# Order of the output and of the opening terms in the first MoE of a fused attention and MoE kernel

## Chip, cores and metric

The kernel runs on one core of one Trainium2 chip. The metric is the device time of one execution in microseconds (us); lower is better.

## What is computed

```python
def reference(q, k, v, f, ...):
    # attention: B=4, H=8, S=576, D=64
    s = q @ k^T / sqrt(D) + decay(f)           # decay: differences of cumsum(log f); causal
    x = softmax(s) @ v                         # then rows (B*S, H*D) = (2304, 512)
    # first MoE, d_ff 768
    h = maximum(maximum(x @ w1, x @ w2), x @ w3)
    x = h @ w_out                              # (2304, 512)
    # second MoE, d_ff 2048
    h = x @ w_in
    P = a[0] + a[1]*h + a[2]*h*h + a[3]*h*h*h
    Q = 1 + |b[0]|*|h| + |b[1]|*h*h
    return (P / (Q + 1e-6)) @ moe2_w_out
```

## The kernel before

Every product of two fp32 matrices is made of a high and a low part of each operand: three matmuls (high with low, high with high, low with high) are summed in PSUM, the accumulator of TensorE, which has eight banks. The x, hh and xo below therefore are pairs: ACT copies the sum to the high part, and VectorE (or GpSimd) subtracts that from the sum, which gives the low part.

**Attention.** Heads go in pairs, four to a batch (hp 0 to 3). The 576 queries of a batch fall in two groups g, of 320 and 256 columns (GQ). A unit is one head of a pair in one group. One step of the main loop works on three units: scores of the newest (L388, L389, two banks of ps_s; VectorE L390 adds the mask and frees the bank, ACT L396 takes the exponential), transposes of the one before (L428, three banks of ps_t), product with v of the one before that (L444, one bank of ps_o). After a pair's second head, ACT L451 and VectorE L452 make x, one tile for each head pair dc, batch and group. tk and tq (L335) are transposes of keys and queries of a later pair.

**First MoE.** For each batch and group there are 22 units of work (moe1_units): 18 of moe1_h, for six chunks fc of d_ff and three weights j, and four of moe1_o, one for each part dc of the 512 output rows. A unit of moe1_h has 12 matmuls (four head pairs, three terms: L476, L477, L478) on a bank of ps_h, which has two. ACT L482 copies the first weight's result to m, VectorE L484 takes the maximum with the second and third; then ACT L488 and GpSimd (VectorE in the tail, L490) make the chunk's hh. A unit of moe1_o has 18 matmuls on x2p (six chunks, three terms: L502, L503, L504), an eviction to xo (ACT L507, VectorE L508; xo has two buffers), and a store to x2d in DRAM (L57). The function fill hands these units out between the steps of the attention of the next batch. The order that each engine then runs is set by a scheduler, which works on the written order; so a written change moves instructions on all engines.

**Tail.** The last batch's two groups (b = 3) have no attention beside them. tail["n"] is set at L649: hbank then takes banks of four kinds in turn. Beside these units w_in is converted to a high and a low part, in 32 pieces, two for each of 16 column blocks: SP loads a piece (L167, a ring of six buffers), ACT L181 takes the magnitude, VectorE does four steps (L186, L187, L188, L191), ACT L197 copies the high part, GpSimd L200 makes the low one. **Second MoE.** It follows (hq, L732 to L734; oo, L781 to L783), with x2h and x2l and x loaded from x2d.

The two places that the change touches, as they were:

```python
for dc in reversed(range(NDC)):        # moe1_h: newest head pair first
...
for fc in range(NF1):                  # moe1_o: one part dc, all six chunks
```

Of the kernel before, what the change touches and what calls it, by code (L numbers as in the profile page):

```python
# [9 lines left out]
F32R = mybir.dt.float32r  # L10
# [14 lines left out]
GQ = [(0, 320), (320, 576)]  # L25
# [12 lines left out]
def kernel(  # L38
    ctx: ExitStack, tc: tile.TileContext, q, k, v, f, w1, w2, w3, w_out, m2_in, m2_out, m2_a, m2_b, out
):  # L40
    nc = tc.nc
# [4 lines left out]
    P = 128  # L46
    NDC = DM // P
    NF1 = FF1 // P
# [4 lines left out]
    def r32(ap):  # L53
        return ap.bitcast(F32)

    def move(dst, src):
        return nc.sync.dma_start(r32(dst), r32(src))  # L57
# [4 lines left out]
    mpool = ctx.enter_context(tc.tile_pool(name="mpool", bufs=1, side="left"))  # L62
# [47 lines left out]
    for a, z in GQ:  # L110
        part = slice(a, z)
# [350 lines left out]
    def hbank(name):  # L462
        pool, tag = ps_h, "h"
        if tail["n"] is not None:
            pool, tag = TAILP[tail["n"] % len(TAILP)]
            tail["n"] += 1
        return pool.tile([P, 512], F32, name=name, tag=tag)

    def moe1_h(b, g, fc, j):
        w = GQ[g][1] - GQ[g][0]  # L470
        nm_ = f"{b}_{g}_{fc}"
        xs = [xt[b, dc, g] for dc in range(NDC)]
        wh, wl = w1t[fc]
        hp_ = hbank(f"h{j}_{nm_}")
        for dc in reversed(range(NDC)):
            nc.tensor.matmul(hp_[:, :w], wh[:, j, dc], xs[dc][:, 1], start=(dc == NDC - 1), stop=False)  # L476
            nc.tensor.matmul(hp_[:, :w], wh[:, j, dc], xs[dc][:, 0], start=False, stop=False)  # L477
            nc.tensor.matmul(hp_[:, :w], wl[:, j, dc], xs[dc][:, 0], start=False, stop=(dc == 0))  # L478
        with tc.high_priority():
            nxt = mpool.tile([P, 320], F32, name=f"m{j}_{nm_}", tag="mx", bufs=3)  # L480
            if j == 0:
                nc.scalar.activation(nxt[:, :w], hp_[:, :w], AF.Copy)  # L482
            else:
                nc.vector.tensor_tensor(nxt[:, :w], cur[0][:, :w], hp_[:, :w], op=ALU.max)  # L484
            cur[0] = nxt
            if j == 2:
                hh = mpool.tile([P, 2, 320], F32R, name=f"hh_{nm_}", tag="hh", bufs=6)
                nc.scalar.activation(hh[:, 0, :w], nxt[:, :w], AF.Copy)  # L488
                eng = nc.gpsimd if tail["n"] is None else nc.vector
                eng.tensor_tensor(hh[:, 1, :w], nxt[:, :w], r32(hh[:, 0, :w]), op=ALU.subtract)  # L490
                hs[b, g, fc] = hh

    def moe1_o(b, g, dc):
        lo, hi = GQ[g]
        w = hi - lo
        nm_ = f"{b}_{g}_{dc}"
        xp = hbank(f"x2p_{nm_}")
        ds_ = slice(dc * P, (dc + 1) * P)
        for fc in range(NF1):
            hh = hs[b, g, fc]  # L500
            woh, wol = wot[fc][:, 0, ds_], wot[fc][:, 1, ds_]
            nc.tensor.matmul(xp[:, :w], woh, hh[:, 0, :w], start=(fc == 0), stop=False)  # L502
            nc.tensor.matmul(xp[:, :w], wol, hh[:, 0, :w], start=False, stop=False)  # L503
            nc.tensor.matmul(xp[:, :w], woh, hh[:, 1, :w], start=False, stop=(fc == NF1 - 1))  # L504
        with tc.high_priority():
            xo = mpool.tile([P, 2, 320], F32R, name=f"xo_{nm_}", tag="xo", bufs=2)
            nc.scalar.activation(xo[:, 0, :w], xp[:, :w], AF.Copy)  # L507
            nc.vector.tensor_tensor(xo[:, 1, :w], xp[:, :w], r32(xo[:, 0, :w]), op=ALU.subtract)  # L508
            move(x2d[:, dc, :, b * S + lo : b * S + hi], xo[:, :, :w])

    def moe1_units(b, g):
        return [lambda fc=fc, j=j: moe1_h(b, g, fc, j) for fc in range(NF1) for j in range(3)] + [
            lambda dc=dc: moe1_o(b, g, dc) for dc in range(NDC)
        ]


# [83 lines left out]
    for step in range(len(slots) + 2):  # L600
# [4 lines left out]
        if u is not None and u.pair.n + 1 < len(pairs):  # L605
            n = u.pair.n + 1
# [4 lines left out]
        if o:  # L611
            o.attend()
            if step in ready:
                queue.append((step, [x for bg in ready[step] for x in moe1_units(*bg)]))
# [82 lines left out]
    a0, a1, a2, a3, b0, _, b1, one = (ab[:, i : i + 1] for i in range(8))  # L697
# [161 lines left out]
```

## Time and profile before

| what | us |
|---|---|
| median of 3 runs | 954.58 |
| lowest, highest | 954.29, 955.71 |
| profiled execution | 954.83 |
| its span | 953.0 |
| TensorE busy | 932.1 |
| VectorE busy | 723.2 |
| ACT busy | 649.0 |
| GpSimd busy | 239.7 |

The span runs from the first instruction to the last; the 1.8 us between it and the time of the execution lie around it. A busy time is the time in which an engine worked at anything. PE is TensorE, DVE is VectorE, POOL is GpSimd, SPq is the queue in which SP issues transfers. The mean granted clock of TensorE is 0.995. The first MoE of batch 3 runs from about 475 to 554 us, the second MoE from there to the end.

### The profile page before, as it was taken

Reading aid. Unit: us, or ns where it says so; the run is one execution under the profiler, and the core shown is the slowest. Engines: PE = TensorE matmul, PEld = TensorE weight load, DVE = VectorE, ACT = ScalarE, POOL = GpSimd, SP = SyncE. Lnnn points to the kernel's source line nnn. Section 1 sums busy time; section 2 is a strip of 40 time slices with the busy share of each in tenths; the row PEclk is TensorE's granted clock in tenths of the full one; section 3 lists DMA queues with packets and bytes.
Section 4 is the critical chain, followed back from the end, with each engine's and each line's share of the span. In section 5 each row is a group of like instructions: output and inputs, shape, how many; then the busy total and the mean of one; then the engine's idle time right before and its main releaser. Section 6 shows DMA issues by size and latency. Waiting matters only on the chain.

```text
span 953.0 us, 16820 instructions
## 1 busy us (share of the span) xinstructions
PE 932.1 (98%) x5780; PEld 825.9 (87%) x5780; DVE 723.2 (76%) x1692; ACT 649.0 (68%) x1542; POOL 239.7 (25%) x392
## 2 busy tenths in 40 slices
PE   6999999999999999999999999999999999999998
PEld 4768899988999999999999988888888888899997
DVE  8578865556777776524397969888988988899996
ACT  6798777777777677546354567667666666777765
POOL 4344444444555455414132400000000000000000
PEclk9988999999999999999999999999999999999999
DMA  7864332123555564220245386011002102100000
GB/s 192 218 191 119 98 84 58 44 77 107 154 148 167 153 174 140 75 78 2 72 140 188 122 300 231 1 45 45 0 1 67 45 1 67 44 1 1 34 1 34
DMA packets 125743, 88.53 MB, mean 93 GB/s; under 512 B 74573, under 2 KB 110425, under 8 KB 125657
## 3 DMA queue, kind: packets, MB, share of 16 engines
q1 hardware_dynamic: 125656, 87.45, 30.6%
q8 instruction: 46, 0.75, 0.3%
q14 instruction: 41, 0.33, 0.1%
HBM read 64.73 MB, written 22.69 MB: 92 GB/s over the span
## 4 chain that ended last, share of the span: by engine, by line
PE 79%; DVE 12%; ACT 5%; issue 2%; DMA 2%; SPq 0%; ACTq 0%; DVEq 0%
PE hq L734 7%; PE oo L782 7%; PE oo L783 7%; PE hq L732 7%; PE hq L733 7%; PE oo L781 7%; PE h L476 5%; PE h L477 5%; PE h L478 5%; PE tp L428 5%; PE o L444 5%; PE s L388 2%; PE s L389 2%; PE x2p L502 2%; PE x2p L504 2%
## 5 line engine op out<-in xcount | busy, mean ns | idle before, releaser
L476 PE MATMUL h<-x,w1h 128*128 128x320 f32 (+1 forms) x576 | 175.4, 305 | 2.1 <-DVE x L452 1.3
L477 PE MATMUL h<-x,w1h 128*128 128x320 f32 (+1 forms) x576 | 171.8, 298 | 0.0
L478 PE MATMUL h<-x,w1l 128*128 128x320 f32 (+1 forms) x576 | 171.3, 298 | 0.0
L476 PEld LDWEIGHTS h<-x,w1h 128*128 128x128 f32 x576 | 109.3, 190 | 4.0 <-DVE m L484 1.9
L782 PE MATMUL oo<-wp,gh 128*128 128x512 f32 x288 | 112.6, 391 | 0.0
L781 PE MATMUL oo<-wp,gh 128*128 128x512 f32 x288 | 112.0, 389 | 0.0
L741 ACT ACTIVATE s<-hq 128x512 f32<-128x512 f32 (+1 forms) x80 | 44.3, 554 | 97.3 <-PE hq L734 97.2
L477 PEld LDWEIGHTS h<-x,w1h 128*128 128x128 f32 x576 | 109.3, 190 | 0.7 <-issue 0.5
L478 PEld LDWEIGHTS h<-x,w1l 128*128 128x128 f32 x576 | 109.1, 190 | 0.2 <-issue 0.2
L783 PE MATMUL oo<-wp,gl 128*128 128x512 f32 x288 | 109.1, 391 | 0.0
L396 ACT ACTIVATE e<-e,st 128x64 f32<-128x64 f32 (+4 forms) x160 | 88.9, 557 | 28.9 <-DVE st L390 26.5
L408 POOL TENSOR_SCALAR e<-e,rs 128x64 f32<-128x64 f32 (+4 forms) x144 | 76.2, 545 | 80.7 <-DVE rs L402 71.0
L390 DVE CUSTOM_DVE_ANT_0 e<-s,mask 128x320 f32<-128x320 f32 (+3 forms) x160 | 67.2, 432 | 32.4 <-PE s L389 21.2
L430 ACT ACTIVATE pt<-tp 128x384 f32<-128x384 f32 (+3 forms) x160 | 70.3, 469 | 15.3 <-PE tp L428 14.2
L744 DVE SCALAR_TENSOR_TENSOR s<-s,ab,u 128x512 f32<-128x512 f32 (+1 forms) x80 | 55.7, 697 | 32.2 <-ACT u L742 32.0
L428 PE MATMUL tp<-ident,e 128*128 128x128 f32 (+1 forms) x480 | 77.0, 279 | 0.0
L734 PE MATMUL hq<-x,wil 128*128 128x512 f32 (+1 forms) x192 | 69.8, 364 | 0.0
L732 PE MATMUL hq<-x,wih 128*128 128x512 f32 (+1 forms) x192 | 69.8, 363 | 0.0
L733 PE MATMUL hq<-x,wih 128*128 128x512 f32 (+1 forms) x192 | 69.6, 363 | 0.0
L783 PEld LDWEIGHTS oo<-wp,gl 128*128 128x128 f32 x288 | 54.1, 188 | 11.3
L782 PEld LDWEIGHTS oo<-wp,gh 128*128 128x128 f32 x288 | 54.0, 188 | 10.6
L781 PEld LDWEIGHTS oo<-wp,gh 128*128 128x128 f32 x288 | 54.1, 188 | 10.4
(133 smaller groups left out, 2433.7 us busy)
## 6 DMA issues: line engine op xcount, KB each, us to landing
raw_w<-in_moe_w_dram SPq DMA_DIRECT2D x18, 512.0 KB
raw_wp<-in_moe_w_out_dram SPq DMA_DIRECT2D x32, 256.0 KB
wpd<-wp SPq DMA_DIRECT2D x32, 256.0 KB
raw_wi<-in_moe_w_in_dram SPq DMA_DIRECT2D x32, 256.0 KB
wp<-wpd SPq DMA_DIRECT2D x10, 768.0 KB
x2d<-xo SPq DMA_DIRECT2D x16, 320.0 KB
out_dram<-ob SPq DMA_DIRECT2D x18, 256.0 KB
kn<-in_k_dram SPq DMA_DIRECT2D x32, 128.0 KB
```

Of the source, the lines that this page charges most:

```text
L396: nc.scalar.activation(e[:nr], e[:nr], AF.Exp, bias=m, scale=-1.0, accum_out=l)
L408: nc.gpsimd.tensor_scalar(e, e, self.rs[:, 1, j : j + 1], 0.0, op0=ALU.mult, op1=ALU.add)
L428: nc.tensor.transpose(tp[:kr, dst : dst + P], self.e[i][:, Q0[c] : Q1[c]], ident)
L476: nc.tensor.matmul(hp_[:, :w], wh[:, j, dc], xs[dc][:, 1], start=(dc == NDC - 1), stop=False)
L477: nc.tensor.matmul(hp_[:, :w], wh[:, j, dc], xs[dc][:, 0], start=False, stop=False)
L478: nc.tensor.matmul(hp_[:, :w], wl[:, j, dc], xs[dc][:, 0], start=False, stop=(dc == 0))
L732: nc.tensor.matmul(hp_[:, :w], wih[:, dc, fs], xh, start=(dc == 0), stop=False)
L733: nc.tensor.matmul(hp_[:, :w], wih[:, dc, fs], xl, start=False, stop=False)
L734: nc.tensor.matmul(hp_[:, :w], wil[:, dc, fs], xh, start=False, stop=(dc == NDC - 1))
L781: nc.tensor.matmul(o, g[0][:, ts_], wh_, start=(fc == 0), stop=False)
L782: nc.tensor.matmul(o, g[0][:, ts_], wl_, start=False, stop=False)
L783: nc.tensor.matmul(o, g[1][:, ts_], wh_, start=False, stop=(fc == NF2 - 1))
```

## The change

It has two parts. In moe1_h, the unit that opens a batch from the second on (first group, first chunk, first weight) takes its 12 terms in the opposite order: oldest head pair first, and of the newest one the term with x's low part last. Units of the output work differently: moe1_out(b, g, 0) makes chunks 0 to 4 of parts 0 and 1, moe1_out(b, g, 1) makes chunk 5 of both and evicts them, and the third and fourth make parts 2 and 3 as before. Lines behind the change are four higher in moe1_h, and L502 to L504, L507 and L508 become L506 to L508, L516 and L517.

```diff
--- before.py
+++ after.py
@@ -472,10 +472,12 @@
         xs = [xt[b, dc, g] for dc in range(NDC)]
         wh, wl = w1t[fc]
         hp_ = hbank(f"h{j}_{nm_}")
-        for dc in reversed(range(NDC)):
-            nc.tensor.matmul(hp_[:, :w], wh[:, j, dc], xs[dc][:, 1], start=(dc == NDC - 1), stop=False)
-            nc.tensor.matmul(hp_[:, :w], wh[:, j, dc], xs[dc][:, 0], start=False, stop=False)
-            nc.tensor.matmul(hp_[:, :w], wl[:, j, dc], xs[dc][:, 0], start=False, stop=(dc == 0))
+        opens = b > 0 and (g, fc, j) == (0, 0, 0)
+        terms = [t_ for dc in reversed(range(NDC)) for t_ in ((wh, dc, 1), (wh, dc, 0), (wl, dc, 0))]
+        if opens:
+            terms.reverse()
+        for n, (w_, dc, part) in enumerate(terms):
+            nc.tensor.matmul(hp_[:, :w], w_[:, j, dc], xs[dc][:, part], start=(n == 0), stop=(n == len(terms) - 1))
         with tc.high_priority():
             nxt = mpool.tile([P, 320], F32, name=f"m{j}_{nm_}", tag="mx", bufs=3)
             if j == 0:
@@ -490,27 +492,47 @@
                 eng.tensor_tensor(hh[:, 1, :w], nxt[:, :w], r32(hh[:, 0, :w]), op=ALU.subtract)
                 hs[b, g, fc] = hh
 
-    def moe1_o(b, g, dc):
-        lo, hi = GQ[g]
-        w = hi - lo
-        nm_ = f"{b}_{g}_{dc}"
-        xp = hbank(f"x2p_{nm_}")
+    xps = {}
+
+    def moe1_o(b, g, dc, fcs):
+        w = GQ[g][1] - GQ[g][0]
+        if fcs[0] == 0:
+            xps[dc] = hbank(f"x2p_{b}_{g}_{dc}")
+        xp = xps[dc]
         ds_ = slice(dc * P, (dc + 1) * P)
-        for fc in range(NF1):
+        for fc in fcs:
             hh = hs[b, g, fc]
             woh, wol = wot[fc][:, 0, ds_], wot[fc][:, 1, ds_]
             nc.tensor.matmul(xp[:, :w], woh, hh[:, 0, :w], start=(fc == 0), stop=False)
             nc.tensor.matmul(xp[:, :w], wol, hh[:, 0, :w], start=False, stop=False)
             nc.tensor.matmul(xp[:, :w], woh, hh[:, 1, :w], start=False, stop=(fc == NF1 - 1))
+
+    def moe1_x(b, g, dc):
+        lo, hi = GQ[g]
+        w = hi - lo
+        xp = xps[dc]
         with tc.high_priority():
-            xo = mpool.tile([P, 2, 320], F32R, name=f"xo_{nm_}", tag="xo", bufs=2)
+            xo = mpool.tile([P, 2, 320], F32R, name=f"xo_{b}_{g}_{dc}", tag="xo", bufs=2)
             nc.scalar.activation(xo[:, 0, :w], xp[:, :w], AF.Copy)
             nc.vector.tensor_tensor(xo[:, 1, :w], xp[:, :w], r32(xo[:, 0, :w]), op=ALU.subtract)
             move(x2d[:, dc, :, b * S + lo : b * S + hi], xo[:, :, :w])
 
+    def moe1_out(b, g, n):
+        every = range(NF1)
+        if n == 0:
+            for dc in range(2):
+                moe1_o(b, g, dc, every[:-1])
+        elif n == 1:
+            for dc in range(2):
+                moe1_o(b, g, dc, every[-1:])
+                moe1_x(b, g, dc)
+        else:
+            moe1_o(b, g, n, every)
+            moe1_x(b, g, n)
+
     def moe1_units(b, g):
         return [lambda fc=fc, j=j: moe1_h(b, g, fc, j) for fc in range(NF1) for j in range(3)] + [
-            lambda dc=dc: moe1_o(b, g, dc) for dc in range(NDC)
+            lambda n=n: moe1_out(b, g, n) for n in range(NDC)
         ]
```

In the lists of the order that follow, a row is an instruction, or some alike, as its engine meets them: line, operation, output, inputs, shape. A name's last number counts the tiles; those ahead of it are group and chunk (hh), group and part (x2p, xo), batch, group and chunk (h, m), head and group (o, x), or the column block of w_in (cv_wi, raw_wi).

TensorE at the opening of batch 1, before, from o of the last head pair on:

```order
L444 MATMUL o_1_0_3016<-pt_128,v_2724 64x320 x2
L444 MATMUL o_1_0_3016<-pt_128,v_2724 64x256 x2
L444 MATMUL o_1_0_3016<-pt_128,v_2724 64x128 x2
L335 MATMUL tq_0_2962<-ident,qn_2621 128x128 x3
L476 MATMUL h_1_0_0_3223<-x_1_0_3023,w1h_173 128x320
L477 MATMUL h_1_0_0_3223<-x_1_0_3023,w1h_173 128x320
L478 MATMUL h_1_0_0_3223<-x_1_0_3023,w1l_174 128x320
L476 MATMUL h_1_0_0_3223<-x_1_0_2636,w1h_173 128x320
```

and with the change, first behind the last output matmuls of batch 0, then from the same o on:

```order
L508 MATMUL x2p_1_3_3131<-hh_1_5_2949,wo_1441 128x256
L480 MATMUL h_1_0_0_3223<-x_1_0_1912,w1l_174 128x320
L480 MATMUL h_1_0_0_3223<-x_1_0_1912,w1h_173 128x320 x2
L480 MATMUL h_1_0_0_3223<-x_1_0_2249,w1l_174 128x320
L480 MATMUL h_1_0_0_3223<-x_1_0_2249,w1h_173 128x320 x2
L480 MATMUL h_1_0_0_3223<-x_1_0_2636,w1l_174 128x320
L480 MATMUL h_1_0_0_3223<-x_1_0_2636,w1h_173 128x320 x2
L444 MATMUL o_1_1_2798<-pt_130,v_2342 64x256 x8
```

```order
L444 MATMUL o_1_0_3025<-pt_128,v_2724 64x320 x2
L444 MATMUL o_1_0_3025<-pt_128,v_2724 64x256 x2
L444 MATMUL o_1_0_3025<-pt_128,v_2724 64x128 x2
L335 MATMUL tq_0_2962<-ident,qn_2621 128x128 x3
L388 MATMUL s_1_11_1_1_3077<-k1s_1370,q1s_1432 128x256
L389 MATMUL s_1_11_1_1_3077<-k2s_1371,q2s_1433 128x256
L480 MATMUL h_1_0_0_3223<-x_1_0_3032,w1l_174 128x320
L480 MATMUL h_1_0_0_3223<-x_1_0_3032,w1h_173 128x320
L335 MATMUL tq_1_2972<-ident,qn_2621 128x128 x2
L480 MATMUL h_1_0_0_3223<-x_1_0_3032,w1h_173 128x320
L480 MATMUL h_1_0_0_3265<-x_1_0_3032,w1h_173 128x320 x2
```

Nine of the opening unit's terms moved ahead of o_1_1; behind o_1_0 and tq_0 now stand two scores, two terms with x's high part, two transposes, and the term with the low part.

VectorE in the tail, first group of batch 3, from the second maximum of the last chunk on, before:

```order
L484 TENSOR_TENSOR m_3_0_5_7141<-m_3_0_5_7106,h_3_0_5_7128 128x320
L191 SCALAR_TENSOR_TENSOR cv_wi_8_7279<-raw_wi_8_7191,cv_wi_8_7279 128x256
L484 TENSOR_TENSOR m_3_0_5_7176<-m_3_0_5_7141,h_3_0_5_7163 128x320
L490 TENSOR_TENSOR hh_0_5_7178<-m_3_0_5_7176,hh_0_5_7178 128x320
L508 TENSOR_TENSOR xo_0_0_7220<-x2p_0_0_7201,xo_0_0_7220 128x320
L508 TENSOR_TENSOR xo_0_1_7263<-x2p_0_1_7244,xo_0_1_7263 128x320
L508 TENSOR_TENSOR xo_0_2_7306<-x2p_0_2_7287,xo_0_2_7306 128x320
```

and with the change:

```order
L486 TENSOR_TENSOR m_3_0_5_7141<-m_3_0_5_7106,h_3_0_5_7128 128x320
L191 SCALAR_TENSOR_TENSOR cv_wi_8_7279<-raw_wi_8_7191,cv_wi_8_7279 128x256
L186 TENSOR_SCALAR cv_wi_8_7312<-cv_wi_8_7312 128x256
L187 TENSOR_SCALAR cv_wi_8_7312<-cv_wi_8_7312 128x256
L186 TENSOR_SCALAR cv_wi_9_7322<-cv_wi_9_7322 128x256
L188 SCALAR_TENSOR_TENSOR cv_wi_8_7312<-raw_wi_8_7233,cv_wi_8_7312 128x256
L486 TENSOR_TENSOR m_3_0_5_7176<-m_3_0_5_7141,h_3_0_5_7163 128x320
L187 TENSOR_SCALAR cv_wi_9_7322<-cv_wi_9_7322 128x256
L191 SCALAR_TENSOR_TENSOR cv_wi_8_7312<-raw_wi_8_7233,cv_wi_8_7312 128x256
L188 SCALAR_TENSOR_TENSOR cv_wi_9_7322<-raw_wi_9_7243,cv_wi_9_7322 128x256
L492 TENSOR_TENSOR hh_0_5_7178<-m_3_0_5_7176,hh_0_5_7178 128x320
L191 SCALAR_TENSOR_TENSOR cv_wi_9_7322<-raw_wi_9_7243,cv_wi_9_7322 128x256
```

Eight conversion steps of blocks 8 and 9 moved ahead of xo_0_0, four of them between the two m, three between the last m and hh_0_5.

SP's queue in the tail, where those blocks are loaded, before:

```order
L167 DMA raw_wi_8_7191<-in_moe_w_in_dram 128x2x256
L57 DMA x2h_1_7872<-x2d 128x512
L57 DMA x2l_1_7873<-x2d 128x512
L57 DMA x2h_2_7876<-x2d 128x512
L57 DMA x2l_2_7877<-x2d 128x512
L57 DMA x2d<-xo_0_0_7220 128x2x320
L57 DMA x2d<-xo_0_1_7263 128x2x320
L167 DMA raw_wi_8_7224<-in_moe_w_in_dram 128x2x256
L167 DMA raw_wi_9_7234<-in_moe_w_in_dram 128x2x256
L167 DMA raw_wi_9_7267<-in_moe_w_in_dram 128x2x256
```

and with the change:

```order
L167 DMA raw_wi_8_7191<-in_moe_w_in_dram 128x2x256
L167 DMA raw_wi_8_7233<-in_moe_w_in_dram 128x2x256
L167 DMA raw_wi_9_7243<-in_moe_w_in_dram 128x2x256
L57 DMA x2h_1_7872<-x2d 128x512
L57 DMA x2l_1_7873<-x2d 128x512
L57 DMA x2h_2_7876<-x2d 128x512
L57 DMA x2l_2_7877<-x2d 128x512
L57 DMA x2d<-xo_0_0_7256 128x2x320
L57 DMA x2d<-xo_0_1_7263 128x2x320
L167 DMA raw_wi_9_7267<-in_moe_w_in_dram 128x2x256
L167 DMA raw_wi_10_7277<-in_moe_w_in_dram 128x2x256
```

The second load of block 8 and the first of block 9 moved ahead of the loads of x2h and x2l and of the stores of xo_0_0 and xo_0_1.

## Rows read from the trace of the kernel before

**Rows 1.** The page: span, and each engine's busy time and instructions.
```profile
span 953.0 us, 16820 instructions
...
PE 932.1 (98%) x5780; PEld 825.9 (87%) x5780; DVE 723.2 (76%) x1692; ACT 649.0 (68%) x1542; POOL 239.7 (25%) x392
```

**Rows 2.** By stretches: us, busy PE, PEld, DVE, ACT, POOL, PEclk, DMA, GB/s.
```profile
500.00:525.00 25.00, 23.45 (x172) 23.07 (x170) 17.89 (x47) 11.16 (x29) 6.94 (x9) 1.00 0.59 188
525.00:550.00 25.00, 23.52 (x190) 22.70 (x189) 23.52 (x63) 12.20 (x34) 9.69 (x13) 1.00 0.35 108
575.00:600.00 25.00, 25.00 (x112) 20.70 (x111) 23.94 (x38) 18.65 (x31) 0.00 (x0) 1.00 0.46 171
```

**Rows 3.** TensorE's waits, 127 to 954 us: sum, times, longest.
```profile
PE x2p L502 <- ACT hh L488: 2.3, 3, 1.5
PE h L476 <- DVE x L452: 1.3, 1, 1.3
PE x2p L502 <- DVE xo L508: 0.9, 2, 0.6
PE x2p L504 <- DVE hh L490: 0.7, 1, 0.7
PE s L388 <- DVE st L390: 0.4, 2, 0.2
```

**Rows 4.** Timeline, opening of batch 1: start, us, engine, instruction, [idle before <- releaser].
```profile
211.99 0.49 DVE L390 CUSTOM_DVE_ANT_0 e<-s,mask 128x320 f32<-128x320 f32 x1
...
220.22 0.77 ACT L396 ACTIVATE e<-e,st 128x576 f32<-128x576 f32 x1
...
220.98 0.43 ACT L451 ACTIVATE x<-o 128x320 fp32r<-128x320 f32 x1
...
221.44 0.49 DVE L452 TENSOR_TENSOR x<-o,x 128x320 fp32r<-128x320 f32 x1 [0.65 <-ACT x L451]
...
221.99 0.42 PE L476 MATMUL h<-x,w1h 128*128 128x320 f32 x1 [1.31 <-DVE x L452]
```

**Rows 5.** Timeline of PE, batch 1, first group, output part 2.
```profile
285.21 0.41 PE L502 MATMUL x2p<-hh,wo 128*128 128x320 f32 x1 [0.63 <-DVE xo L508]
```

**Rows 6.** Timeline, tail, batch 3, first group: output and last hh.
```profile
504.35 0.31 PE L502 MATMUL x2p<-hh,wo 128*128 128x320 f32 x1
...
504.50 0.31 PE L503 MATMUL x2p<-hh,wo 128*128 128x320 f32 x1
...
509.14 0.47 DVE L484 TENSOR_TENSOR m<-m,h 128x320 f32<-128x320 f32 x1
...
509.65 0.47 ACT L488 ACTIVATE hh<-m 128x320 fp32r<-128x320 f32 x1
...
510.15 0.67 DVE L490 TENSOR_TENSOR hh<-m,hh 128x320 fp32r<-128x320 f32 x1 [0.54 <-ACT hh L488]
...
510.17 0.42 PE L502 MATMUL x2p<-hh,wo 128*128 128x320 f32 x1 [1.54 <-ACT hh L488]
```

**Rows 7.** Timelines of SP's queue, ACT and DVE: loads of w_in, conversion behind them.
```profile
478.41 23.36 SPq L167 DMA_DIRECT2D raw_wi<-in_moe_w_in_dram  x12
...
513.25 2.43 SPq L167 DMA_DIRECT2D raw_wi<-in_moe_w_in_dram  x4
...
516.84 0.44 ACT L181 ACTIVATE cv_wi<-raw_wi 128x256 f32<-128x256 f32 x1 [1.66 <-DMA raw_wi<-in_moe_w_in_dram]
...
517.32 0.29 DVE L186 TENSOR_SCALAR cv_wi<-cv_wi 128x256 f32<-128x256 f32 x1 [1.60 <-ACT cv_wi L181]
```

**Rows 8.** Two conversion steps, 475 to 550 us: ns min/median/max, starts, form.
```profile
L186 DVE TENSOR_SCALAR cv_wi<-cv_wi x31: 278/284/870, 475.3 to 544.2; 128x256 f32<-128x256 f32 x31
...
L188 DVE SCALAR_TENSOR_TENSOR cv_wi<-raw_wi,cv_wi x32: 409/425/970, 475.5 to 545.9; 128x256 int32<-128x256 int32 x32
```

**Rows 9.** Timeline of PE, tail, batch 3, second group: first and last output matmul.
```profile
542.76 0.28 PE L502 MATMUL x2p<-hh,wo 128*128 128x256 f32 x1
...
553.78 0.28 PE L504 MATMUL x2p<-hh,wo 128*128 128x256 f32 x1
553.90 0.40 PE L732 MATMUL hq<-x2h,wih 128*128 128x512 f32 x1
```

## Prediction

> **What bounds the kernel now.** I read the page's totals first: TensorE is busy for 932.1 of 953.0 us [rows 1], so no order of the same matmuls can take more than its idle time, and all the matmuls stay. Then the table by stretches: in the second MoE TensorE has no gap at all (25.00 of 25.00), in the tail of the first MoE it has 1.55 and 1.48 us of them in two stretches of 25 us, at the full granted clock of 1.00, 2.4 GHz [rows 2]. The time there is lost to waits, not to the clock. Third, the list of TensorE's waits from 127 us on, which is the part of the program that is reordered: 2.3 + 1.3 + 0.9 + 0.7 + 0.4 = 5.6 us in nine waits [rows 3]. The list counts the idle time ahead of an instruction; the start of a matmul behind a wait is late by some 0.16 us more than that (1.54 listed, 1.70 late, worked out below), so nine waits cost about 7 us. That is the whole stake, 0.7% of the kernel. Last the timelines around those waits. The smallest difference that a measurement here can tell from none is about 0.2%, 1.9 us.
>
> **What the change leaves alone.** TensorE runs the same 5780 matmuls, and the copies, subtractions and transfers are the same in number; only the order differs. TensorE's pitch from one 320-column matmul to the next is 504.50 − 504.35 = 0.15 us whatever bank it writes [rows 6]; changing banks every 15 matmuls I cost at nothing. The second MoE keeps its order and has no gap to fill, so what the first MoE gives or takes comes through to the end in full.
>
> **The opening of a batch.** Before, batch 1's first unit starts with the newest head pair's low part. The chain is: ACT ends an exponential of 0.77 us, copies o to x (220.98, 0.43), VectorE subtracts (221.44, 0.49), and the matmul starts at 221.99 after 1.31 us of idling, late by about 1.5 [rows 4]. In the change nine of the unit's twelve terms (1.3 us of matmuls) stand some 8 us earlier, and behind o of the last head pair come three transposes, two score matmuls (0.12 each, the pitch for 256 columns [rows 9]) and two terms that need only ACT's copy, then two transposes, and the low part last. ACT's copy now precedes the last exponential of 0.77, so x's two parts come that much sooner, while TensorE, having done its nine terms already, also arrives 1.3 sooner, with 0.3 of scores to cover. My hand count of the new wait is 0.3 to 1.1; a **gain of 0.9** (0.4 to 1.4). Batches 2 and 3 open in the same new order, but no wait of L476 other than batch 1's is in the list [rows 3], so they are worth nothing.
>
> **Side by side, outside the tail.** What the pair wants to hide is the last chunk's hh. But none of the L502 waits on hh before the tail: the three add up to 2.3, of which the tail has 1.54 at 510.17 and two smaller ones near the end [rows 3, 6]. The cover from the last h matmul to the first use of hh's last chunk (matmuls between them in the two orders, times the pitch) grows there from 3.5–5.4 us to 4.7–7.0, which buys nothing. What can go wrong is at the bank: parts 0 and 1 now end together, so part 2 waits for an eviction that started later. In batch 0 the stretch between the end of part 0 and the start of part 2 shrinks from 2.2 to 1.3 us for the first group of queries; it was idle for 0.3 there (0.9 less the 0.63 of batch 1 [rows 3, 5]), and ACT and VectorE keep the order of that eviction, so I leave it unchanged. In batch 1's first group, where part 2 was idle for 0.63 us behind VectorE's xo [rows 5], the list now puts a slot's scores and transposes ahead of it (7.2 us instead of 2.0). That wait goes, but nine score groups now stand close together on two banks, each freed by a VectorE step such as the 0.49 us one of [rows 4], where TensorE writes a pair of scores in some 0.3 (two pitches). Nine steps of 0.49 against nine of 0.3 is 1.7 late, less what stands between: I take 2.0 for the new stalls of the whole group against 1.3 now, a **loss of 0.7** (0 to 1.6). In batch 1's second group the scores spread out and the two waits on VectorE's st, 0.4 [rows 3], go: a **gain of 0.4** (0 to 0.5).
>
> **Tail, batch 3, first group.** Before, the output starts at 504.35 and 28 matmuls of 0.147 last until 508.47; the first use of hh's last chunk starts at 510.17, 1.70 late. It waits for VectorE's m (509.14, 0.47) and ACT's hh (509.65, 0.47); hh's low part follows at 510.15 [rows 6]. The change adds two matmuls of cover (0.29). But it pulls eight conversion steps of w_in ahead on VectorE, four between the last two m (behind an L191 that stood there already), three before hh's low part and one right behind it. L186, L187, L186 and L188 thus precede the last m, and the L186 on piece 9 needs that piece's load. SP now issues two of these loads before the x2h and x2l loads, where before they stood behind the stores of xo. SP's earlier loads went out every 23.36 / 12 = 2.0 us and the last ended at 478.41 + 23.36 = 501.8; so by the ring's pace I put the two at 503.7 and 505.7. From issue to ACT's first step took 516.84 − 513.25 = 3.6, and that step 0.44 [rows 7]: piece 9 is ready near 509.8. Then L186 and L188 (medians 0.284 and 0.425 [rows 8]) and m: 510.5 to 511.1 for its start plus copying, against 509.14, hence hh 1.1 to 1.5 later. TensorE has used 0.29 of that; hh's low part stands behind three more steps (some 1.1 us) and costs another 0.3. A **loss of 1.4** (0.7 to 2.4).
>
> **Tail, second group.** From 542.76 to 553.90 pass 11.14 us for 72 matmuls at the pitch 553.90 − 553.78 = 0.12, 8.64 [rows 9]: 2.5 us are waits on hh. VectorE is the late one: it is busy for 23.52 of 25 us [rows 2]. It lost its time earlier: in the stretch before, it worked 17.89 of 25 us, with 1.66 us on ACT and then 1.60 on VectorE spent waiting for the load issued at 513.25 [rows 7]. With the loads out 8 us earlier, VectorE has eight steps of 0.28 to 0.43 (2.9 us) behind it by 520. That lead is more than the 2.5 us, so hh is ready in time: a **gain of 2.4** (1.0 to 2.5). For small shifts elsewhere between 127 and 545 us, where every engine's order differs, I add **0.3** (−0.3 to +1.1), two waits of the size of the smaller ones in [rows 3].
>
> **The sum:** −0.9 + 0.7 − 0.4 + 1.4 − 2.4 + 0.3 = −1.3 us. The profiled execution took 954.83 us, 1.8 outside the span of 953.0; the median of the runs is 954.58, so the sum gives 953.5 on the first and **953.3** on the second.
>
> **The rivals.** (1) *The targets all hit.* The score cluster of batch 1 is spread by what stands between, the loads for piece 9 land in time, and TensorE is served at once: −1.4 − 0.6 − 0.5 − 0.2 − 2.5 + 0.5 = −4.7, that is 949.9. For it: rows show that both tail waits hang on VectorE's backlog, and the change works it off. Against: VectorE's list puts more ahead of the first group's hh, not less. It decides from piece 9 ready by 508.5. Chance 0.22. (2) *Waits only change place.* VectorE's lead is used up by ACT's and GpSimd's part of the conversion, so that the second group gains 1.0 rather than 2.4: +0.1, 954.7. For it: ACT and GpSimd do steps of every piece too, and VectorE's stand behind ACT's. Against: VectorE's 7 idle us of 500 to 525 are largely one late load [rows 2, 7]. Chance 0.15. (3) *The load becomes the bound, and it is slower.* In VectorE's queue a step on piece 9 now precedes the last m. If its buffer comes free, or the transfer lands, 2.4 us later than I put it (512.2 rather than 509.8), VectorE stands still with m behind it, hh and TensorE with it: the first group loses 3.8 instead of 1.4, and of VectorE's lead 0.5 are left, so the second gains 0.5: −0.9 + 0.7 − 0.4 + 3.8 − 0.5 + 0.3 = +3.0, 957.6. It is slower by what can be told from about 511.5 on. For it: DMA is at its densest in the tail right here, 0.59 [rows 2], and the wait for a load of the same kind was 1.66; against: the pace and landing of the earlier loads. Chance 0.14. (4) *VectorE's steps stretch.* L186 takes 0.284 in the median but up to 0.870, L188 up to 0.970 [rows 8]; GpSimd is busy for 6.94 of 25 us there [rows 2], so about two of eight steps would meet it and lose 0.6 each: −1.3 + 1.2 = −0.1, 954.5. It decides by how many of the eight are long. Chance 0.08. The Trainium skill, page "SBUF — State Buffer", section "Who interferes with whom", has VectorE and GpSimd share a pair of ports as an exclusive lock, the second of two such instructions blocked until the first ends; the long L186 and L188 agree with it. By that rule, were all eight blocked, the first group would lose some 4.7 more; the medians at the minimum say that most are not.
>
> **How the numbers follow.** My forecast has the chance 0.41; its own range, from the bounds of its terms taken half way, is 951.6 to 955.0. Of it a third lies below 952.7, two thirds within 0.2%. With rival 1 wholly faster, rivals 2 and 4 mostly the same, and most of rival 3 slower: faster 0.14 + 0.22 = 0.36; same 0.27 + 0.14 + 0.08 + 0.01 = 0.50; slower the remaining 0.14. The range reaches from rival 1 to short of rival 3's full price: 950.0 to 956.6.
>
> **What would show it.** Right: the wait of L476 (now L480) on VectorE's x below 1 us; L502 (now L506) on hh near 547 gone and the last x2p within 8.8 us of the first; at 510, a longer wait than 1.54; VectorE well above 17.89 of 25 us in 500 to 525; a load of piece 9 before 507. Wrong: the second group's waits still there with VectorE earlier; new waits of several us on st in batch 1; any wait inside the second MoE.

## The result and the profile after

| | median us | lowest, highest | runs |
|---|---|---|---|
| before | 955.47 | 954.29, 957.81 | 6 |
| changed | 960.29 | 959.60, 961.30 | 6 |

The change makes the kernel slower: ratio 1.0052, 95% interval 1.0041 to 1.0064, some 4.9 us. Forecast were 953.3 us and a range up to 956.6. The profiled execution of the changed kernel took 960.78 us. Its page:

```profile
span 959.0 us, 16819 instructions
...
PE 935.4 (98%) x5780; PEld 826.6 (86%) x5780; DVE 721.7 (75%) x1692; ACT 647.2 (67%) x1542; POOL 238.2 (25%) x392
```

Against [rows 1], TensorE is *busier* by 3.3 us with the same 5780 matmuls, and the span is longer by 6.0. The first is a sign of the clock: a matmul at the lower clock counts as busy for longer. TensorE's waits from 127 us on (sum, times, longest), to be held against [rows 3]:

```profile
PE s L388 <- DVE st L390: 2.8, 6, 0.7
PE x2p L506 <- ACT hh L490: 2.5, 2, 1.7
PE h L480 <- ACT x L451: 0.7, 1, 0.7
PE tp L428 <- POOL e L408: 0.7, 2, 0.4
PE h L480 <- DVE m L486: 0.5, 1, 0.5
```

The wait of the scores for VectorE's st grew from 0.4 to 2.8 us. Where, the table by stretches says (busy PE, PEld, DVE, ACT, POOL, then PEclk), 275 to 310 us, the outputs of batch 1's first group, of the kernel before:

```profile
275.00:310.00 35.00, 34.33 (x267) 31.93 (x264) 26.73 (x85) 26.26 (x77) 18.12 (x33) 1.00 0.54 160
```

and of the changed one:

```profile
275.00:310.00 35.00, 32.29 (x225) 28.18 (x225) 26.23 (x87) 25.09 (x76) 18.78 (x34) 0.95 0.52 153
```

Idle time of 0.67 us became 2.71, and the clock's mean fell to 0.95. The timeline of PE there, changed kernel:

```profile
284.98 0.36 PE L388 MATMUL s<-k1s,q1s 128*128 128x192 f32 x1 [0.65 <-DVE st L390]
...
287.00 0.36 PE L388 MATMUL s<-k1s,q1s 128*128 128x192 f32 x1 [0.68 <-DVE st L390]
...
290.70 0.47 PE L388 MATMUL s<-k1s,q1s 128*128 128x448 f32 x1 [0.44 <-DVE st L390]
...
291.98 0.49 PE L388 MATMUL s<-k1s,q1s 128*128 128x320 f32 x1 [0.61 <-DVE st L390]
...
292.66 3.59 PE L444 MATMUL o<-pt,v 128*64 128x256 f32 x20
```

The first four rows are of the ten score groups that stand closely together, from 284.98 to 292.26 us (the prediction counted nine). VectorE, ahead of the first of them, was at this:

```profile
279.21 1.12 DVE L191 SCALAR_TENSOR_TENSOR cv_wp<-raw_wp,cv_wp 128x256 int32<-128x256 int32 x1
...
282.47 0.68 DVE L186 TENSOR_SCALAR cv_wp<-cv_wp 128x256 f32<-128x256 f32 x1
283.19 0.29 DVE L187 TENSOR_SCALAR cv_wp<-cv_wp 128x256 int32<-128x256 int32 x1
283.51 0.43 DVE L188 SCALAR_TENSOR_TENSOR cv_wp<-raw_wp,cv_wp 128x256 int32<-128x256 int32 x1
283.98 0.42 DVE L191 SCALAR_TENSOR_TENSOR cv_wp<-raw_wp,cv_wp 128x256 int32<-128x256 int32 x1
284.43 0.48 DVE L390 CUSTOM_DVE_ANT_0 e<-s,mask,st 128x256 f32<-128x256 f32 x1
```

The step that frees a bank of scores, 0.48 long, stands behind a whole piece of the conversion of the second MoE's output weights (wp, by the same lines as that of w_in). The second wait (287.00) comes a step later: the score step that frees its bank stands on VectorE behind L402, which waited for ACT, and ACT had stood for 3.71 us at its own part of the conversion:

```profile
284.48 0.42 ACT L197 ACTIVATE wp<-cv_wp 128x256 fp32r<-128x256 f32 x1 [3.71 <-DVE cv_wp L191]
...
286.38 0.17 DVE L402 RECIPROCAL rs<-rs 128x2 f32<-128x2 f32 x1 [0.53 <-ACT rs L401]
286.46 0.47 DVE L390 CUSTOM_DVE_ANT_0 e<-s,mask 128x320 f32<-128x320 f32 x1
```

And then, by stretches of 2 us, the clock:

```profile
290.00:292.00 2.00, 0.95 (x5) 0.37 (x4) 2.00 (x10) 2.00 (x8) 0.00 (x0) 1.00 0.00 0
292.00:294.00 2.00, 2.00 (x9) 1.10 (x10) 2.00 (x10) 2.00 (x7) 1.90 (x4) 0.54 0.39 139
294.00:296.00 2.00, 2.00 (x16) 1.22 (x12) 0.86 (x3) 1.25 (x5) 2.00 (x5) 0.60 0.35 115
296.00:298.00 2.00, 2.00 (x20) 1.83 (x17) 0.49 (x2) 0.77 (x3) 1.12 (x2) 1.00 0.71 221
```

From 284 to 292 TensorE was busy for 5.28 of 8 us (1.21, 1.32, 1.80 and this 0.95); behind that the granted clock went to its lower level, 1.2 GHz, and the 20 matmuls of o took 3.59 us. In the kernel before the same 20 took 2.17:

```profile
293.72 2.17 PE L444 MATMUL o<-pt,v 128*64 128x256 f32 x20
```

So 1.4 us of the loss is the clock's on this group alone.

**Lost time.** To compare kernels whose order differs, I add up, over all matmuls, the distance from its start to the next start less the median distance behind a matmul of the same kind in the kernel before. That counts waits and the lower clock alike, in us:

| kernel | 218–275 | 275–310 | 310–475 | 475–572 | ratio (95%) |
|---|---|---|---|---|---|
| before | 2.8 | 2.2 | 3.9 | 4.3 | |
| changed | 3.7 | 6.3 | 5.4 | 3.6 | 1.0052 (1.0041–1.0064) |
| e1 opening alone | 3.6 | 4.8 | 5.1 | 4.6 | 1.0051 (1.0033–1.0069) |
| e2 side by side alone | 3.1 | 3.6 | 4.6 | 7.0 | 1.0029 (1.0015–1.0044) |
| e3 not in batch 1's first group | 3.4 | 5.0 | 5.3 | 6.9 | 1.0083 (1.0061–1.0105) |
| e4 there alone | 2.9 | 4.3 | 3.5 | 3.5 | 1.0014 (1.0001–1.0027) |
| f1 changed, no VectorE steps | 2.8 | 2.0 | 3.7 | 3.7 | 0.9980 (0.9969–0.9992) |
| f2 before, no VectorE steps | 3.0 | 1.8 | 5.0 | 7.3 | 1.0026 (1.0013–1.0039) |
| f3 side by side in batch 3 alone | 3.0 | 2.8 | 4.0 | 5.4 | 1.0007 (0.9992–1.0021) |
| f4 opening in batches 2, 3 alone | 3.0 | 2.6 | 4.1 | 4.5 | 0.9994 (0.9980–1.0008) |
| g1 opening, no VectorE steps | 2.9 | 0.6 | 7.3 | 3.9 | 1.0007 (0.9994–1.0020) |
| g2 before, conversion later | 2.8 | 0.7 | 8.8 | 5.8 | 1.0041 (1.0027–1.0055) |
| g3 changed, conversion later | 2.6 | 1.4 | 8.9 | 7.2 | 1.0072 (1.0056–1.0087) |
| g4 side by side in last group alone | 3.0 | 2.4 | 4.1 | 5.7 | 1.0006 (0.9994–1.0017) |
| h1 changed, five pieces without steps | 3.5 | 2.1 | 5.2 | 7.9 | 1.0054 (1.0037–1.0070) |
| h2 pace, a trifle earlier | 7.3 | 0.7 | 5.9 | 4.3 | 1.0075 (1.0055–1.0095) |
| h3 pace, a trifle later | 3.8 | 1.2 | 3.7 | 5.5 | 1.0031 (1.0019–1.0043) |

The changed kernel's differences to before, 0.9 + 4.1 + 1.5 − 0.8 = 5.7, make up the 6.0 of the spans. Each row is one profiled execution (e2's was among the longest of its 12 runs, 961.2 us of 956.5 to 961.2). f3, f4 and g4 keep the order of the kernel before up to 475 us and show how far it repeats: 2.4 to 2.8 where before had 2.2. Of the three, f4 alone keeps the order of the tail too, 4.5 against 4.3. Ratios are against the kernel before on the same chip (medians of 955.80 to 957.22 us there).

The changed kernel is not alone in losing the clock. In eight of these profiles (changed, f2, f3, g1, g2, h1, h2, h3) it fell to the lower level between 127 and 572 us, once each and twice in g2, and by the same measure each such stretch holds 1.3 to 1.7 us of the lost time. The profile of the kernel before has none there.

### The profile page after: what moved, and what is told of

It is laid out like the page before. It is cut to its first block, busy times and chain, and to the rows that moved or that the text cites. A ratio compares the mean times of both kernels' runs of the same rounds, so it can differ in the third digit from the quotient of the medians.

```text
span 959.0 us, 16819 instructions
## 1 busy us (share of the span) xinstructions
PE 935.4 (98%) x5780; PEld 826.6 (86%) x5780; DVE 721.7 (75%) x1692; ACT 647.2 (67%) x1542; POOL 238.2 (25%) x392
## 4 chain that ended last, share of the span: by engine, by line
PE 54%; DVE 5%; DMA 2%; issue 1%; ACT 1%; POOL 0%; SPq 0%; ACTq 0%; DVEq 0%; POOLq 0%
PE hq L754 7%; PE hq L756 7%; PE oo L804 7%; PE hq L755 7%; PE oo L805 7%; PE oo L803 7%; PE h L480 6%; PE o L444 1%; DVE cv_wi L188 1%; PE tp L428 1%; DVE cv_wi L186 1%; DMA x2d<-xo 1%; PE x2p L506 1%; PE x2p L508 1%; DMA raw_wi<-in_moe_w_in_dram 1%
## 5 line engine op out<-in xcount | busy, mean ns | idle before, releaser
L480 PE MATMUL h<-x,w1h 128*128 128x256 f32 (+1 forms) x1152 | 244.3, 302 | 1.4 <-DVE m L486 1.1
L480 PEld LDWEIGHTS h<-x,w1h 128*128 128x128 f32 x1152 | 186.9, 190 | 4.6 <-DVE m L486 2.6
L486 DVE TENSOR_TENSOR m<-m,h 128x320 f32<-128x320 f32 (+1 forms) x96 | 43.1, 449 | 24.9 <-PE h L480 12.6
L428 PEld LDWEIGHTS tp<-ident,e 128*128 128x128 f32 (+1 forms) x480 | 55.7, 134 | 6.7 <-issue 1.9
```

Source lines behind the costliest of these rows:

```text
L428: nc.tensor.transpose(tp[:kr, dst : dst + P], self.e[i][:, Q0[c] : Q1[c]], ident)
L480: nc.tensor.matmul(hp_[:, :w], w_[:, j, dc], xs[dc][:, part], start=(n == 0), stop=(n == len(terms) - 1))
```

## The experiments

**The two edits apart.** e1 makes the outputs as before (moe1_out calls moe1_o and moe1_x for one part), e2 sets `opens = False`. e3 and e4 choose the place:

```diff
+        if (b, g) == (1, 0):      # e3; e4: if (b, g) != (1, 0), and opens = False
+            moe1_o(b, g, n, every)
+            moe1_x(b, g, n)
+        elif n == 0:
-        if n == 0:
```

> The opening order alone, outputs as before. Theory (the loss comes from the side-by-side output in batch 1's first group, where nine score groups meet two banks and the clock then falls): no loss here, -1.0 to +0.7 us against the kernel before, clock 1.00 from 275 to 300 us. Rival 'the opening starts it' (the new order of the opening pushes the later work together): +3 to +5 us. Rival 'a bit everywhere': +0.5 to +1.5 us.

> The side-by-side outputs alone, opening as before. Theory: +4 to +6 us against the kernel before, the clock below 0.97 in 275 to 300 us, waits on VectorE's st there of 2 us or more. Rival 'the opening starts it': -2 to +1 us. Rival 'a bit everywhere' (each of eight groups loses some 0.6 at the banks): +3 to +5 us, but spread over the groups and the clock at 1.00.

> The whole change, except that batch 1's first group makes its outputs part by part as before. Theory: the loss goes, -2.5 to +1.0 us against the kernel before, the clock 1.00 from 275 to 300 us. Rival 'the opening starts it': +4 to +5 us. Rival 'a bit everywhere': +3 to +4.5 us.

> The kernel before, with side by side in batch 1's first group alone. Theory: nearly the whole loss, +3.5 to +5.5 us against the kernel before, the clock below 0.97 in 275 to 300 us. Rival 'the opening starts it': 0 to +1 us. Rival 'a bit everywhere': +0.3 to +1 us.

My theory fell in its simple form. The opening alone costs as much as the whole change, 0.51%, though its order has no close run of scores; side by side in batch 1's first group alone costs only 0.14%; and leaving it out there makes the kernel slower still, 0.83%. The clock stayed at 1.00 from 275 to 310 us in e2 and e4, where I had expected it to fall. Both edits raise the lost time from 275 to 310 us, by 2.6 and 1.4 us; that this comes close to the 4.1 of both together is chance as far as is known, for e1's waits are others, and over the whole kernel they don't add (0.51% and 0.29% against 0.52%). In e1 the places are others, but the engine is the same. Its timelines of PE, ACT and DVE:

```profile
282.71 0.68 DVE L186 TENSOR_SCALAR cv_wp<-cv_wp 128x256 f32<-128x256 f32 x1
283.42 0.29 DVE L187 TENSOR_SCALAR cv_wp<-cv_wp 128x256 int32<-128x256 int32 x1
283.75 0.43 DVE L188 SCALAR_TENSOR_TENSOR cv_wp<-raw_wp,cv_wp 128x256 int32<-128x256 int32 x1
284.21 0.48 DVE L390 CUSTOM_DVE_ANT_0 e<-s,mask,st 128x256 f32<-128x256 f32 x1
...
284.74 0.78 ACT L396 ACTIVATE e<-e,st 128x576 f32<-128x576 f32 x1 [3.72 <-DVE st L390]
...
285.94 0.44 ACT L516 ACTIVATE xo<-x2p 128x320 fp32r<-128x320 f32 x1
...
286.41 0.49 DVE L517 TENSOR_TENSOR xo<-x2p,xo 128x320 fp32r<-128x320 f32 x1 [1.23 <-ACT xo L516]
...
286.95 0.42 PE L506 MATMUL x2p<-hh,wo 128*128 128x320 f32 x1 [1.15 <-DVE xo L517]
```

VectorE comes to the score at 284.21, late behind conversion steps; ACT, in its order, stands for 3.72 us at that score's exponential, with the eviction of x2p behind it; TensorE waits for the bank. Its other long wait there hangs on a load: the score step stands behind a conversion step that waited for ACT, and ACT for the piece.

```profile
291.67 0.44 ACT L181 ACTIVATE cv_wp<-raw_wp 128x256 f32<-128x256 f32 x1 [1.70 <-DMA raw_wp<-in_moe_w_out_dram]
...
292.15 0.29 DVE L186 TENSOR_SCALAR cv_wp<-cv_wp 128x256 f32<-128x256 f32 x1 [0.94 <-ACT cv_wp L181]
292.36 0.48 DVE L390 CUSTOM_DVE_ANT_0 e<-s,mask 128x320 f32<-128x320 f32 x1
...
292.91 0.41 PE L388 MATMUL s<-k1s,q1s 128*128 128x320 f32 x1 [0.91 <-DVE st L390]
```

**VectorE's conversion steps.** f1 (changed), f2 (before) and g1 (opening alone) leave out VectorE's four steps for the second MoE's output weights; h1 leaves them out for five of 32 pieces:

```diff
         def bits():
+            if pin:        # h1: if nm_ in ("wp_4_1", "wp_5_0", "wp_5_1", "wp_6_0", "wp_6_1"):
+                return
```

> The changed kernel without VectorE's four steps (L186, L187, L188, L191) in the conversion of the second MoE's output weights, which runs beside batch 1's first MoE; those weights are then wrong, all else is computed. To be read against its twin, the kernel before without the same steps. Theory (what is lost between 275 and 360 us are score and eviction steps that stand late on VectorE behind these conversion steps, some of them stretched to 1.1 us): the waits between 275 and 360 us shrink from about 5 us to under 1.5, and the kernel is within -2 to +1.5 us of its twin. Rival 'banks' (the new order of TensorE itself waits on banks and on the two xo buffers): +3.5 to +5 us above the twin, as with the steps.

> The kernel before without the same four VectorE steps in the conversion of the second MoE's output weights (those weights are wrong): the twin. Theory and rival alike: -2.5 to 0 us against the kernel before, since its own waits of 275 to 350 us sum to 1.5 us.

> The opening order alone (the kernel that lost 0.5%), without VectorE's four conversion steps of the second MoE's output weights (those weights are wrong). Twin: the kernel before without the same steps. Theory (the loss of the opening is made by those steps on VectorE and what waits behind them): TensorE's lost time between 218 and 475 us falls from 13.5 us to 8 to 10 us (8.8 in the kernel before), and the kernel is not above its twin by more than 1 us. Rival (the opening's own chain or the banks): lost time stays at 12 us or more, +3 to +5 us above the twin.

> The changed kernel without VectorE's four steps for five of the 32 pieces of the second MoE's output weights, those that run from 276 to 295 us (these weights are wrong). TensorE's order stays that of the changed kernel up to the outputs of batch 1's first group, and nine score groups stand there as closely as before. Theory (the conversion steps between the score steps on VectorE make the waits): TensorE's lost time from 275 to 310 us falls from 6.3 us to 3 or less, the clock stays at 1.00 there. Rival (the scores' own steps on VectorE and two banks are enough, as the prediction priced it): it stays above 5 us.

At the place in question the theory held each time: lost time from 275 to 310 us fell from 6.3 to 2.0 in f1 and to 2.1 in h1, and from 4.8 to 0.6 in g1. h1 is the sharpest, for its TensorE meets nine score groups as closely as the changed kernel does (output part 2 comes ahead of the tenth, so from there on the order is another); its row for 275 to 310 us:

```profile
275.00:310.00 35.00, 34.34 (x264) 31.80 (x261) 22.27 (x71) 26.75 (x81) 20.21 (x35) 1.00 0.62 180
```

TensorE's idle time is back at 0.66 us and the clock at 1.00, with VectorE 4.0 us less busy. Up to the ninth group TensorE idled for 2.1 us in the changed kernel and for 0.67 in h1. So score groups on two banks don't lose that time by themselves; the conversion steps between them do. The tenth group's wait and the lower clock behind it come where the two orders differ. f1 is 0.2% faster than the kernel before and 0.46% faster than its twin, more than expected; f2, that twin, was not the gain of 0 to 2.5 that I expected but slower by 0.26%, and that in the tail (7.3 against 4.3), far behind the steps left out. h1 as a whole gained nothing over the changed kernel: its tail lost 7.9. g1 lost 7.3 from 310 to 475 us (1.7 of it at the lower clock, from 344.6 us on), so that from 218 to 475 it comes to 10.8 instead of the 8 to 10 expected; against its twin f2 it is within the bound. A stretch was cured each time, and the order behind it, drawn anew, lost elsewhere.

**The conversion later.** g2 (before) and g3 (changed) begin that conversion at slot 42:

```diff
-    CONV2, EARLY = (32, 0.25), 12
+    CONV2, EARLY = (42, 0.25), 12
```

> The kernel before, with the conversion of the second MoE's output weights begun at slot 42 instead of 32, so that it lies beside batches 1's end and 2 and not beside batch 1's outputs. Theory: batch 1's waits go, new ones can come where it lies now: -1.5 to +2 us against the kernel before.

> The changed kernel with the same later conversion. Theory (VectorE's conversion steps beside batch 1's outputs make the loss): the lost time of TensorE from 275 to 310 us falls from 6.3 us to under 3, no fall of the clock there, and the kernel gains 2 to 5 us against the changed kernel: -2 to +3 us against the kernel before. Rival (order and banks): +4 us or more against the kernel before, with the waits still between 284 and 292 us.

From 275 to 310 us the loss fell as the theory has it, to 0.7 and 1.4. But from 310 to 475, beside the conversion where it now lies, the loss rose to 8.8 and 8.9. As to the whole time, the expectations failed for g2 (at most +2 us; 0.41% are 3.9) and for g3 (at most +3; 0.72% are 6.9), which is slower than the changed kernel. That the conversion makes the loss in the new place too is not shown: g1, which has none of its steps on VectorE, lost 7.3 in the same stretch, and g2's longest waits there, 1.2 us in all, are for GpSimd's e.

**The tail, and the other openings.** f3 is side by side for `b == B - 1` alone, g4 for `(b, g) == (B - 1, 1)` alone, both with `opens = False`; f4 opens for `b > 1` alone, without side by side.

> Side by side in the last batch alone (both groups), opening as before; everything up to 475 us keeps its order. Theory: the part of the change that pays, by the tail's traces: first group 0 to +0.5, second -1.2 to -2.4, in all -2.4 to -0.5 us against the kernel before. Rival 'the tail loses too' (the second kernel with side by side alone lost 2.6 us in the tail's first group): 0 to +3 us.

> Side by side in the last group of the last batch alone. Theory (the second group of the tail gains because the first group pulls VectorE's conversion and its loads ahead, not by the two parts side by side): the gain of the second group fails to come, its waits stay at 1.5 to 3 us, -0.5 to +0.5 us against the kernel before. Rival (side by side itself hides the last hh): the second group's waits fall under 1 us, -2.5 to -1 us.

> The opening order in batches 2 and 3 alone, no side by side. The order of VectorE, ACT and GpSimd stays, and of TensorE's only the terms of two units swap. Theory (the loss of the opening is that of batch 1's, through what stands behind it): -0.8 to +0.8 us against the kernel before. Rival 'the reversed terms cost by themselves': +1 us or more.

f4 is the kernel before within 0.1%: reversed terms by themselves cost nothing that can be measured. f3 as a whole gained nothing (+0.07%), where I had expected −2.4 to −0.5 us. Both of its groups move the way that the prediction traced, but the first loses more than forecast. One wait of the outputs for ACT's hh is left from 475 us on, in the first group, longer than the 1.54 of [rows 6]; the second group has none:

```profile
PE x2p L506 <- ACT hh L490: 2.9, 1, 2.9
PE x2p L508 <- DVE hh L492: 0.2, 1, 0.2
```

Lost time up to 530 us rose from 1.8 to 5.0, and behind it fell from 2.5 to 0.3: −2.2 given, +3.2 taken. Of the 3.2, the longer wait is 1.3 (2.85 against 1.54), close to the 1.4 forecast, and the clock some 1.4 more: it fell behind that wait. The rows of f3 for 503 to 515 and 514 to 516 us:

```profile
503.00:515.00 12.00, 8.93 (x55) 8.40 (x54) 11.83 (x29) 5.67 (x14) 5.06 (x7) 0.95 0.57 175
...
514.00:516.00 2.00, 2.00 (x9) 2.00 (x9) 1.16 (x3) 0.82 (x3) 0.73 (x2) 0.50 0.00 0
```

VectorE was busy for 11.83 of the 12 us: what came ahead of the last m were its own conversion steps, and it did not stand waiting for the load of piece 9, by which the prediction had timed that m. In g4, where the first group pulls nothing ahead, the waits stay:

```profile
PE x2p L506 <- ACT hh L490: 2.6, 4, 1.5
PE x2p L508 <- DVE hh L492: 1.0, 2, 0.7
```

So the second group's gain comes from VectorE's lead, not from side by side hiding the last hh. How much of that lead is only TensorE's own delay in the first group, no run tells apart.

**An order drawn anew by a change of no meaning.** h2 and h3 change the pace of the first MoE's units by one count:

```diff
-            state["of"] = max(1, NFILL * (ends[at] - step) - 3)
+            state["of"] = max(1, NFILL * (ends[at] - step) - 4)   # h3: - 2
```

> The kernel before, with the first MoE's units handed out a trifle earlier (the pace's constant 3 made 4), no opening order and nothing side by side. A change of no meaning that makes the scheduler draw the order anew from TensorE's row 1027 on. Theory 'any new order of this stretch loses, since the one of before is a good draw': +1 to +6 us against the kernel before. Rival 'only what the change itself does loses': -1 to +1 us.

> The same the other way (3 made 2: units a trifle later). Theory 'any new order loses': +1 to +6 us against the kernel before. Rival 'only the change itself': -1 to +1 us.

Both are slower, by 0.75% and 0.31%, with neither edit in them, and their losses lie elsewhere again: 7.3 in h2 at batch 1's opening, 5.5 in h3 in the tail, 1.7 and 1.5 of these at the lower clock. The count does hand units out earlier or later, so that the pace itself has no part in this is not shown. With the changed kernel, e1 to e4, g2 and g3, these are nine kernels that do all of the work and have a new order from the middle of the program on or earlier: all nine are slower than the kernel before. No version that does all the work beat it.

## Why the prediction was wrong

- **What bounds the kernel** was right, but the stake was taken from one side only. Some 7 us of waits bounded the gain; the loss has no such bound. I read the waits that the order has and not the waits that it was free of.
- **Batch 1's first group**, "a loss of 0.7 (0 to 1.6)", is the step that failed: it measured 4.1. "Nine steps of 0.49 against nine of 0.3" set VectorE's score steps against TensorE's as if nothing stood between them on VectorE. The rows show a whole piece's four conversion steps ahead of one score step, and behind a step of another piece that took 1.12 us; and h1 shows that without such steps the first nine of these score groups cost 0.67 us of idle time instead of 2.1. The order of VectorE in this stretch was to be had beforehand, as that of the tail was. And the sum had no term for the clock, which took 1.4 us of the 4.1 at o.
- **The opening**, "a gain of 0.9", is −0.9, a loss. Its own wait shrank much as forecast, from 1.31 [rows 4] to 0.69 us, now on ACT's x; but a second wait opened behind it, for VectorE's m:

```profile
223.03 0.41 PE L480 MATMUL h<-x,w1l 128*128 128x320 f32 x1 [0.69 <-ACT x L451]
...
229.41 0.56 PE L480 MATMUL h<-x,w1h 128*128 128x320 f32 x2 [0.50 <-DVE m L486]
```

  Worse, e1 shows that these nine matmuls, moved 8 us ahead, made a new order that loses 3.8 us more from 275 to 475 us (2.6 + 1.2). I had costed that at "0.3, small shifts elsewhere".
- **Side by side outside the tail** buys nothing, as the prediction said. **Batch 1's second group**, a gain of 0.4: of the two waits only one, 0.17 us at 343.73, lay there; the other, at 142.82, is batch 0's and stayed. The one did go, but two for GpSimd's e came instead, 0.67 us in all, and 310 to 475 us lost 1.5 more.
- **The tail**, −1.0 forecast, gave −0.8, and that they agree is luck: the first group lost 0.4 more, the second 1.2 less than before, where 1.4 and 2.4 were forecast; and in f3, which enters the tail as the kernel before does, they came to +3.2 and −2.2. The wait at 510.17 [rows 6] and the 2.5 us of [rows 9] became these:

```profile
517.65 0.41 PE L506 MATMUL x2p<-hh,wo 128*128 128x320 f32 x1 [1.66 <-ACT hh L490]
```

```profile
549.88 0.28 PE L506 MATMUL x2p<-hh,wo 128*128 128x256 f32 x1
...
552.33 0.38 PE L506 MATMUL x2p<-hh,wo 128*128 128x256 f32 x1 [0.85 <-ACT hh L490]
...
559.85 0.40 PE L754 MATMUL hq<-x2h,wih 128*128 128x512 f32 x1
```

  9.97 us for the 72 matmuls instead of 11.14. The direction of both terms was right, and f3 and g4 bear it out; what the sum had no term for is the clock behind a wait, which made f3's first group lose 3.2 where the wait alone grew by 1.3. VectorE's 7 idle us of 500 to 525, which rival 2 called largely one late load, were mostly others: in the kernel before, 2.50 and 0.97 us of them stood ahead of the subtractions of xo, 1.60 and 1.33 behind L181. That time in the tail is lost to waits and not to the clock held for the kernel before; in f2, f3, g2, h1 and h3 the clock fell there too.
- **The rivals.** The one on the slow side named a load in the tail; the loss lies 230 us earlier. That VectorE's steps stretch beside GpSimd was a rival for the tail only; in batch 1 it was the first of the late steps. What none of them said is what h2 and h3 show: that a new order with neither edit cost 3 and 7 us.
- **The forecast's own range**, 951.6 to 955.0, does not follow from its working: the bounds of its terms taken half way give 951.9 to 955.8. The result lies outside either.

What stays open: how much of the 4.9 us belongs to the edits and how much to the draw, since no run could freeze the order behind them. That the conversion steps cause the waits of the changed kernel from 285 to 291 us is shown; that a schedule without them elsewhere would make the change pay is not (f1's 0.2% leaves work out).

## What to carry to other kernels

When a scheduler sets the order, an edit of a few instructions is a new order for all engines behind it: price it by VectorE's and ACT's queues wherever matmuls moved together, not only where a wait was to go. Before trusting an edit's gain or loss below 1%, time a change of no meaning that moves as many rows. A wait of TensorE beside a nearly full engine costs once more where the lower clock follows it.

## What the runs showed of the hardware

The clock fell without a long pause: between 284 and 292 us TensorE's longest idle time was 0.68 us, it was busy for two thirds of the time, and yet the next 20 matmuls took 3.59 instead of 2.17 us; the clock was back at 1.00 from 296 us on. In e1 a wait of 1.15 us at 286.95 did not bring it down. It differs between executions of one kernel, too: of the 104 runs of the kernel before beside the experiments, the 33 with a mean granted clock of 0.995 took 955.3 us in the median, the ten at 0.989 took 958.5. So one profile can hold or miss such a fall.

A conversion step of VectorE (L191, median 0.42) lasted 1.12 us while GpSimd ran these two:

```profile
279.17 0.88 POOL L492 TENSOR_TENSOR hh<-m,hh 128x320 fp32r<-128x320 f32 x1
...
280.13 0.46 POOL L328 TENSOR_SCALAR q2s<-q1s 64x256 fp32r<-64x256 f32 x1
```

It began 0.04 us behind the first and ended at 280.33, some 0.3 us behind that one's end. The Trainium skill, page "SBUF — State Buffer", section "Who interferes with whom", says that a VectorE instruction with two inputs in SBUF contends with a GpSimd instruction that reads SBUF, and that the pair of ports between them is an exclusive lock. The trace agrees in kind: the step was held for 0.70 us (1.12 less 0.42), not for all of the 0.88.
